# Moving the last batch's third and fourth X and its Fourier products one part later between the first feed-forward products

## The chip, the cores and the metric

The kernel runs on one core of a Trainium2 chip. The metric is the device time of one execution in microseconds (us). TensorE (PE) does the matrix products and the transposes, PEld is its loading of weights, VectorE is DVE, ScalarE is ACT, GpSimd is POOL, and SyncE (SP) issues most of the DMAs.

## The reference

Two blocks follow each other, all in float32 (the two weight matrices arrive as float64 and are converted on the chip). The first is attention whose heads are mixed before and after the softmax; its result is laid out as rows of 768 values. The second adds to each batch the real part of a Fourier transform over the sequence and over the model width, normalises each row, and applies a feed-forward block.

```
scores = einsum('bhij,hg->bgij', scale * q @ k.T, w_pre)      # batch 8, heads 12, seq 448, dim 64
attn   = softmax(scores)
attn   = einsum('bhij,hg->bgij', attn, w_post)
x      = (attn @ v) as rows (8, 448, 768)
u      = x + real(fft(fft(x, axis=1), axis=2))
un     = (u - mean) / sqrt(var + 1e-6)
out    = u + relu(un @ w_ch1) @ w_ch2                         # 768 -> 3072 -> 768
```

## The kernel before, in words

The kernel has two phases, `mix_phase` and `ffn_phase`.

**The mixing loop.** A batch is cut into 23 steps (GS = 23), so eight batches make TOT = 184 steps; the last batch begins at step f = 161. In a step PE mixes the heads before the softmax (`mx`, L704), VectorE takes the maximum, ScalarE the exponential, POOL scales by the sum, PE mixes again (`po`, L738), VectorE transposes. Work that is not bound to one step lies in lists with due step numbers (`due`, `take`): among them the products with v (`emit_av`, L769), which ScalarE copies into the tile `XT`.

**X, the folds, the Fourier products.** For each batch there are four groups of rows. `emit_x` (L813) transposes a group's `XT` into the tile X by six PE transposes and two ScalarE copies (L516). The groups come in the order of the table AT_X, whose entries are a step and a group number: 0, 1, 3, 2; they are called the first to the fourth X here. Since the Fourier matrices are symmetric, rows and columns are first added to and subtracted from their mirror images on POOL: `fold` puts eight small calls per pair of groups on a list (L834, L839, L848, L849), and after the second pair four more that join the two pairs into `xf` (L855). In the loop the folds are taken a few at a time. A Fourier product over the sequence (`emit_z`, four per batch, L878) needs all of `xf`: whatever folds are still on the list are issued in front of it, and PE then waits for POOL. ScalarE copies its result to `z`. A second product over the width (`emit_s2`, four per batch, L894) follows, whose result VectorE adds to X in four additions (L905, L907), and when both halves are there the rows of `u` are stored in DRAM: by SP (L926), by POOL with an indirect DMA (L917) and one last row by POOL (L923).

**What does not fit into the loop.** For the last batch the late items cannot be hidden under a following batch. `mix_phase` returns them as a list of parts, in the order of their due steps, each with a call that issues it, and a call `fold_rest(n)` that issues the next n folds. A part whose due step is from TOT + 10 = 194 on also first issues the stores that are pending (the list `later`).

**The feed-forward phase** works on seven tiles of 512 rows and six parts of the weights. Each tile has a first and a second half, each of seven products (a product scheme with seven instead of eight, in the order 0, 4, 5, 1, 6, 2, 3). In `first`, each product is six matmuls (L1264) of a `ub` tile (the transposed, normalised rows and their sums; the buffers are named qs, ks or ub) with a weight tile `w1t`, into the PSUM banks psP, psQ or psR; VectorE and ScalarE combine the results to `h` (L1274 to L1293), and VectorE makes sums of `h` (L1310, L1311, L1314, L1325) at the end. In `second`, each product is four matmuls (L1341) of `h` with `w2t`, which VectorE adds to the rows (`ur`, `u`, L1346). While tile t runs, tile t + 1 is prepared: VectorE takes statistics (L1182), POOL turns them into scale and bias in four steps (`power`, L440 to L443, tile `mv`), ScalarE normalises (L1193), PE transposes (L1202), ScalarE copies (L1204) into the next `ub` tiles. SP loads `u` (L1161), `w1t` (L1165) and `w2t` (L1169) and stores the `ub` tiles of tile 0 (L1498).

**The parts in between.** The function `next_part` takes one part from the list. It is called in tile 0 behind the first and second product of `first`, then behind the fourth to seventh product of `second`, and in tile 1 behind the first, fourth, fifth, sixth and seventh product of `first`: eleven times. Behind the second product of tile 0 six folds are issued with `fold_rest(6)`, behind its sixth product all others. The order on PE, DVE, POOL and SP is the order of the code here (`manual_schedule`), and that on ScalarE is a scheduler's; each engine carries out its instructions in its order.

The lines that set which items are left for the parts are the due step of an X of the last batch, and the end of the loop:

```
            at, gi = AT_X[n]
            if b == B - 1 and n > 1:
                at += 2
            due("full", f + at, lambda g=groups[b * NG + gi]: emit_x(g))
...
        while s <= TOT - GS + AT_X[-1][0]:
```

With AT_X = ((17, 0), (23, 1), (28, 3), (31, 2)) the last batch's third X is due at 161 + 30 = 191 and its fourth at 194. The loop runs to 161 + 31 = 192. So the third X is in the loop and the fourth is the first of ten parts.

Of the kernel before, what the change touches and what calls it, by code (L numbers as in the profile page):

```python
# [45 lines left out]
GS = BLOCK_AT[-1]  # L46
# [14 lines left out]
TOT = B * GS  # L61
# [36 lines left out]
         (11, 11, 12), (12, 15, 14))  # L98
AT_AV = ((6, 9, 10), (13, 13, 14), (19, 19, 22), (24, 26, 27))
AT_X = ((17, 0), (23, 1), (28, 3), (31, 2))  # L100
AT_Z = (38, 38, 40, 40)
AT_S = ((41, 44), (47, 48))

# [374 lines left out]
def mix_phase(ctx, tc, rest, ident, q, k, v, w_pre, w_post, u_scr, u_rev, wts, lead):  # L478
# [39 lines left out]
    def flush():  # L518
        while pend:
            pend.pop(0)[1]()  # L520
# [63 lines left out]
    def emit_load_qk(b, xx, nm, y):  # L584

        src = q if nm == "q" else k
        if y == 0 and b == 0 and xx == START[-1]:

            if "raw" not in first:
                first["raw"] = ppv.tile([P, GT, 2 * S], F32, name="Pv", tag="Pv")  # L590
            batches[b]["raw" + nm, xx] = first["raw"][:, nm == "q"].rearrange(
                "p (c x d) -> p c x d", c=C7, x=2)
        elif y == 0:
            batches[b]["raw" + nm, xx] = praw.tile([P, C7, 2, D], F32, name="raw" + nm,
                                                   tag="raw")
        t = batches[b]["raw" + nm, xx]
        for x in range(2):
            eng = nc.gpsimd if b else (nc.sync, nc.scalar if xx == START[0] else nc.gpsimd)[x]
            eng.dma_start(
                out=t[64 * y:64 * y + 64, :, x, :],  # L600
                in_=src[b, 4 * xx + 2 * x + y].rearrange("(p c) d -> p c d", c=C7))
        return True
# [35 lines left out]
    def emit_xpose(b, xx, nm):  # L638
        st = batches[b]
        raw = st.pop(("raw" + nm, xx))  # L640
        w = WQ if nm == "q" else S
        t = pqt.tile([P, 2, w], F32, name=nm + "T", tag=nm + "T")
        st[nm + "T", xx] = t
        rt = _row(t)
        if nm == "q":
            eng = nc.gpsimd if b else nc.vector
            eng.memset(t[:, :, 0:MG], 0.0)
            eng.memset(t[:, :, MG + S:WQ], 0.0)
        evs = []
        for c0, n in ((0, 4), (4, 3)):  # L650
            ps = ms_tile()
            for c in range(n):
                nc.tensor.transpose(
                    ps[:, c * P:(c + 1) * P],
                    raw[:, c0 + c].rearrange("p x d -> p (x d)"), ident[:, :])
            dst = _ap(t, (w - S) // 2 + c0, [[rt, P], [1, n], [w, 2], [C7, 64]])
            src = ps[:, :n * P].rearrange("p (c y t) -> p c y t", c=n, y=2)
            evs.append(lambda dst=dst, src=src, n=n: copy(ENG["tr", nm, n], dst, src))
        return evs

    def emit_qk(n, xx):

        bk = blocks[n]
        st = batches[bk["b"]]
        engs = ENG["QK"] if n > 1 else "ad"
        if "Sb" not in bk:
            bk["Sb"] = psb.tile([P, 6, S], F32, name="Sb", tag="Sb")
        c0, w = bk["r0"] + MG, R * bk["rs"]
        n = 64 + w
        pss = [ms_tile() for _ in range(2)]  # L670
        for y in range(2):
            for o in (64 * y, 64 * y + 32):
                lo = c0 + o - 64 + (0 if y else w)
                hi = min(lo + 32, c0 + w)
                for x in range(2):
                    nc.tensor.matmul(  # L676
                        pss[x][o:o + hi - lo, :S],
                        st["qT", xx][64 * x:64 * x + 64, y, lo:hi],
                        st["kT", xx][64 * x:64 * x + 64, y, :],
                        start=True, stop=True)  # L680
        return [lambda x=x: copy(engs[x], bk["Sb"][:n, 2 * xx + x, :],
                                 pss[x][:n, :S]) for x in range(2)]
# [251 lines left out]
    def due(kind, at, fn):  # L934
        fill[kind].append((at, len(fill[kind]), fn))
# [4 lines left out]
    for b in range(B):  # L940
        f = b * GS
        at_t = [(a, nm, xx) for xx, at in enumerate(AT_T) for nm, a in zip("qk", at)]
        if b == 0:

            for i, xx in enumerate(START):
                for j, nm in enumerate("kq"):
                    for y in range(2):
                        due("none", -40, lambda xx=xx, nm=nm, y=y: emit_load_qk(0, xx, nm, y))
                    due("full", 2 * i + j - 20, lambda xx=xx, nm=nm: emit_xpose(0, xx, nm))
                for n, at in enumerate((2 * i - 18, i - 13)):  # L950
                    due("QK", at, lambda n=n, xx=xx: (emit_qk(n, xx), n))
            for pr in range(3):
                for y in range(2):
                    due("none", -40, lambda pr=pr, y=y: emit_load_v(0, pr, y))
        else:
            f0 = f - GS
            for n, (a, nm, xx) in enumerate(sorted(at_t, key=lambda e: e[0])):
                at, a = (AT_L[n], a) if b > 1 else (AT_L1[n], AT_T1[n])
                for y in range(2):
                    due("none", f0 + at[y],  # L960
                        lambda b=b, xx=xx, nm=nm, y=y: emit_load_rows(b, xx, nm, y))
                due("flip", f0 + a, lambda b=b, xx=xx, nm=nm: emit_flip(b, xx, nm))
        for pr in range(3 if b else 0):
            for y in range(2):
                due("none", f + AT_V[pr][y], lambda b=b, pr=pr, y=y: emit_load_v(b, pr, y))
        for n in range(0 if b else 2, NBL):
            for xx in range(3):
                due("QK", AT_QK0[n][xx] if b == 0 and n in AT_QK0 else
                    f + AT_QK[n][xx] - (GS if n < 3 else 0),
                    lambda n=NBL * b + n, xx=xx: (emit_qk(n, xx), n))  # L970
        for n in range(NG):
            for pr in range(3):
                due("AV", f + AT_AV[n][pr],
                    lambda a=b * NG + n, pr=pr: (emit_av(a, pr), None))
            at, gi = AT_X[n]
            if b == B - 1 and n > 1:
                at += 2
            due("full", f + at, lambda g=groups[b * NG + gi]: emit_x(g))
        for n, at in enumerate(AT_Z):
            due("full", f + at, lambda b=b, n=n: emit_z(b, n // 2, n % 2))  # L980
        for pair in range(2):
            for par in range(2):
                due("full", f + AT_S[pair][par],
                    lambda b=b, pair=pair, par=par: emit_s2(b, pair, par))
    f = (B - 1) * GS
# [35 lines left out]
    s = int(min(v_[0][0] for v_ in fill.values()))  # L1021
    ET = mybir.EngineType
    with tc.manual_schedule(engines={ET.PE, ET.DVE, ET.Activation, ET.Pool}):
        while s <= TOT - GS + AT_X[-1][0]:
            old = len(later)
            n = take("none", s)
            ahead, now = 0 <= s + LM < TOT, 0 <= s < TOT
            for op in ORDERS[ORD[s % GS]]:
                if op == "flush":
                    flush()  # L1030
                elif op in fill:
                    take(op, s)
                elif op == "conv":
                    if s >= 4:
                        wts.deal(1)
                elif op == "gather":
                    if 0 <= s + LG < TOT:
                        if any(e[2] is not None and e[2] <= at_step[s + LG][0] for e in pend):
                            flush()
                        emit_gather(s + LG)  # L1040
                elif op == "scale":
                    if ahead:
                        emit_scale(s + LM)
                    for _ in range(old if s < TOT + 5 else 0):
                        later.pop(0)()

                    if s < TOT - 3:
                        for _ in range(min(len(folds), 1 if n and s > 3 else 2)):
                            folds.pop(0)()
                elif op in ("post", "turn"):  # L1050
                    if now:
                        (emit_postmix if op == "post" else emit_turn)(s)
                elif ahead:
                    (emit_premix if op == "pre" else emit_max if op[0] == "m"
                     else emit_exp)(s + LM, *map(int, op[3:]))
            s += 1
        flush()
        assert not wts.ops
        wts.deal(0)
# [545 lines left out]
```

## Time and profile before

| | us |
|---|---|
| median of 3 runs | 2301.52 |
| lowest and highest of them | 2299.84, 2303.2 |
| the profiled execution's own time | 2302.76 |
| its span, first to last instruction | 2301.0 |
| mean granted TensorE clock | 0.991 |

The profile is of one execution. Times in it are counted from the span's start, so about 1.8 us of the execution's time lie around the span. A row of a time line has the start, the length, the engine, the line, the operation, what it writes and reads, how many instructions it stands for, and in brackets the idle time of the engine ahead of it with what ended it. Matmuls overlap a little, so a row's length is about 0.16 us more than the distance to the start of the next. A line such as L1264 is a line of the kernel before; behind line 100 the changed kernel's lines have numbers one higher.

### The profile page before, as it was taken

Reading aid. Unit: us, or ns where it says so; the run is one execution under the profiler, and the core shown is the slowest. Engines: PE = TensorE matmul, PEld = TensorE weight load, DVE = VectorE, ACT = ScalarE, POOL = GpSimd, SP = SyncE. Lnnn points to the kernel's source line nnn. Section 1 sums busy time; section 2 is a strip of 40 time slices with the busy share of each in tenths; the row PEclk is TensorE's granted clock in tenths of the full one; section 3 lists DMA queues with packets and bytes.
Section 4 is the critical chain, followed back from the end, with each engine's and each line's share of the span. In section 5 each row is a group of like instructions: output and inputs, shape, how many; then the busy total and the mean of one; then the engine's idle time right before and its main releaser. Section 6 shows DMA issues by size and latency. Waiting matters only on the chain. (4 is left out here: it accounts for less than half of the span.)

```text
span 2301.0 us, 60190 instructions
## 1 busy us (share of the span) xinstructions
PE 2235.0 (97%) x22600; PEld 1745.0 (76%) x22600; DVE 1723.4 (75%) x3640; ACT 1141.1 (50%) x3288; POOL 1310.4 (57%) x1805
## 2 busy tenths in 40 slices
PE   6999999999999799999999999999999999999998
PEld 3445555555555567676899999999999999999998
DVE  5778888898888547777777787878778877765545
ACT  4666666667666423231445445444444445434434
POOL 6688888989869522211555455546545645454334
PEclk8999999999999999999999999999999999999999
DMA  7576676666746555658777887878777987795664
GB/s 167 169 186 181 177 198 171 196 182 189 195 152 184 189 181 178 225 186 305 207 178 187 240 220 188 218 185 246 208 187 187 284 184 175 192 255 121 144 147 76
DMA packets 228828, 439.41 MB, mean 191 GB/s; under 512 B 35964, under 2 KB 149558, under 8 KB 228540
## 3 DMA queue, kind: packets, MB, share of 16 engines
q1 hardware_dynamic: 156620, 301.52, 38.5%
q0 software_dynamic: 69632, 133.00, 30.9%
q8 instruction: 181, 2.97, 0.6%
q10 hardware_dynamic: 2288, 1.05, 0.2%
q14 instruction: 107, 0.88, 0.1%
HBM read 213.16 MB, written 143.16 MB: 155 GB/s over the span
## 5 line engine op out<-in xcount | busy, mean ns | idle before, releaser
L1420 POOL DMA_DIRECT2D out_dram<-od x172 | 209.0, 1274 | 260.8 <-DVE od L1408 177.4
L718 ACT ACTIVATE PP<-mx,nmx 128x448 f32<-128x448 f32 x368 | 231.1, 634 | 171.5 <-DVE nmx L711 161.2
L728 POOL TENSOR_SCALAR PP<-PP,rcp 128x448 f32<-128x448 f32 x368 | 234.6, 648 | 138.7 <-DVE rcp L726 105.3
L711 DVE TENSOR_REDUCE nmx<-mx 128x1 f32<-128x448 f32 x368 | 212.6, 615 | 92.1 <-PE mx L704 90.3
L1227 POOL TENSOR_TENSOR hq<-h 128x128 f32<-128x128 f32 (+1 forms) x210 | 130.1, 619 | 255.4 <-ACT h L1286 123.0
L704 PE MATMUL mx<-Kr,kw 60*32 60x448 f32 x2944 | 226.6, 553 | 16.8 <-DMA Kr<-Sb 12.6
L1414 ACT COPY od<-psP 128x192 f32<-128x192 f32 x488 | 156.3, 320 | 171.7 <-PE psP L1386 170.6
L1417 DVE TENSOR_TENSOR od<-od 128x768 f32<-128x768 f32 x210 | 200.5, 968 | 52.5 <-ACT od L1414 52.3
L738 PE MATMUL po<-PP,kw 60*32 60x448 f32 x2944 | 208.4, 541 | 3.1 <-POOL PP L728 2.1
L752 DVE STREAM_TRANSPOSE Pv<-po 128x896 f32<-128x896 f32 x184 | 203.6, 1106 | 8.5 <-PE po L738 5.8
L676 PE MATMUL ms<-kT,qT 64*32 64x448 f32 (+1 forms) x3072 | 196.6, 543 | 3.2 <-ACT qT L516 1.9
L516 ACT COPY Sb<-ms 124x448 f32<-124x448 f32 (+1 forms) x378 | 178.7, 546 | 40.9 <-PE ms L676 28.0
L769 PEld LDWEIGHTS ms<-Pv,vv 64*64 64x64 f32 x5376 | 139.9, 133 | 63.4 <-issue 34.6
L1264 PE MATMUL psP<-ks,w1t 128*128 128x256 f32 x744 | 179.9, 380 | 0.1
L1264 PE MATMUL psP<-qs,w1t 128*128 128x256 f32 x744 | 179.0, 379 | 0.7 <-DVE h L1285 0.7
L769 PE MATMUL ms<-Pv,vv 64*64 64x120 f32 (+1 forms) x5376 | 160.9, 264 | 4.9 <-issue 2.7
L281 POOL TENSOR_SCALAR wst<-wst 128x256 f32<-128x256 f32 (+1 forms) x76 | 118.5, 1567 | 68.5 <-ACT wst L292 67.2
L1264 PEld LDWEIGHTS psP<-ks,w1t 128*128 128x128 f32 x744 | 140.1, 191 | 16.9 <-DVE u L1346 0.7
L1264 PEld LDWEIGHTS psP<-qs,w1t 128*128 128x128 f32 x744 | 139.5, 190 | 17.4 <-DVE h L1285 1.1
L676 PEld LDWEIGHTS ms<-kT,qT 64*32 64x32 f32 (+1 forms) x3072 | 74.1, 106 | 80.6 <-issue 51.4
L1264 PE MATMUL psP<-ub,w1t 128*128 128x256 f32 x528 | 127.1, 379 | 0.6 <-DVE h L1285 0.6
L738 PEld LDWEIGHTS po<-PP,kw 60*32 60x32 f32 x2944 | 71.1, 107 | 72.2 <-issue 54.2
(203 smaller groups left out, 5271.2 us busy)
## 6 DMA issues: line engine op xcount, KB each, us to landing
Kr<-Sb SPq DMA_DIRECT2D x730, 105.0 KB
out_dram<-od POOLq DMA_DIRECT2D x172, 384.0 KB, 7.0
qs<-ub SPq DMA_DIRECT2D x89, 384.0 KB
ks<-ub SPq DMA_DIRECT2D x88, 384.0 KB
ub<-ub SPq DMA_DIRECT2D x79, 384.0 KB
w1t<-w SPq DMA_DIRECT2D x42, 384.0 KB
w2t<-w SPq DMA_DIRECT2D x42, 384.0 KB
raw<-in_moe_w_ch_dram SPq DMA_DIRECT2D x32, 384.0 KB
```

Of the source, the lines that this page charges most:

```text
L516: (nc.scalar.copy if eng == "a" else nc.vector.tensor_copy)(out=out, in_=in_)
L676: nc.tensor.matmul(pss[x][o:o + hi - lo, :S], st["qT", xx][64 * x:64 * x + 64, y, lo:hi], st["kT", xx][64 * x:64 * x + 64, y, :], start=Tr ...
L704: nc.tensor.matmul(mx[x][64 * z + o:64 * z + o + 32, :S], kw1[64 * x:64 * x + KR, o:o + 32], Kr[64 * x:64 * x + KR, z, :], start=True, sto ...
L711: nc.vector.tensor_reduce(nmx[:, :], steps[T]["mx"][x][:, :S], axis=AX.X, op=ALU.max, negate=True)
L718: nc.scalar.activation(steps[T]["PP"][:, x, :], steps[T]["mx"][x][:, :S], ACTF.Exp, bias=steps[T]["nmx", x][:, :], accum_out=steps[T]["den ...
L728: nc.gpsimd.tensor_scalar(PP[:, x, :], PP[:, x, :], rcp[:, x:x + 1], 1.0, op0=ALU.mult, op1=ALU.mult)
L738: nc.tensor.matmul(po[o:o + 32, z, :S], kw2[64 * z:64 * z + KR, y, :], _ap(PP, 64 * z * _row(PP) + 32 * c, [[_row(PP), KR], [S, 2], [64, C ...
L752: nc.vector.transpose(turned[a]["Pv"][:, j, :].rearrange("p (z s) -> p z s", z=2), steps[T]["po"][:, :, :S])
L769: nc.tensor.matmul(pss[y][64 * x:64 * x + 64, :nu * R], st["v", pr][64 * y:64 * y + 64, x, jb * D:(jb + 1) * D], _ap(Pv, 64 * y * rp + 32 ...
L1264: mm = nc.tensor.matmul(p[:, m, :], w1[i][:, kc, m * P:(m + 1) * P], ub[:, kc, :], start=i in (0, 4, 1)[:3 - seed] and m == kc == 0, stop= ...
L1417: eng.tensor_tensor(D[j][:, :, :], D[j][:, :, :], D[k][:, :, :], op=ALU.add)
L1420: nc.gpsimd.dma_start(out=acc[t, r, d], in_=D[j][:, :, :], accum_op=ALU.add)
```

## The change

The last batch's third and fourth X are now due at TOT + AT_END and the step after (191 and 192), with AT_END = 7, and the loop ends ahead of step TOT + AT_END. Its last step is 190, so both are parts, and there are eleven. Since both have due steps below TOT + 10, neither issues pending stores first.

```
+AT_END = 7
...
             at, gi = AT_X[n]
             if b == B - 1 and n > 1:
-                at += 2
+                at = TOT - f + AT_END + n - 2
             due("full", f + at, lambda g=groups[b * NG + gi]: emit_x(g))
...
-        while s <= TOT - GS + AT_X[-1][0]:
+        while s < TOT + AT_END:
```

What this moves is seen in the order of the instructions. First PE, from the end of the mixing loop on, before (L769 is the last product with v, L813 an X, L1264 feed-forward products of tile 0, L878 a Fourier product):

```order
L769 MATMUL ms<-Pv,vv 64x120 x56
L813 MATMUL ms<-ident,XT 113x128 x6
L1264 MATMUL psP<-qs,w1t 128x256 x6
L813 MATMUL ms<-ident,XT 113x128 x6
L1264 MATMUL psR<-qs,w1t 128x256 x6
L878 MATMUL ms<-ts,xf 97x113
L878 MATMUL ms<-ts,xf 97x112
L878 MATMUL ms<-ts,xf 97x113
L878 MATMUL ms<-ts,xf 97x112
L1264 MATMUL psP<-ks,w1t 128x256 x6
L1264 MATMUL psQ<-qs,w1t 128x256 x6
```

And the same place of the changed kernel (its line numbers are one higher):

```order
L770 MATMUL ms<-Pv,vv 64x120 x56
L1265 MATMUL psP<-qs,w1t 128x256 x6
L814 MATMUL ms<-ident,XT 113x128 x6
L1265 MATMUL psR<-qs,w1t 128x256 x6
L814 MATMUL ms<-ident,XT 113x128 x6
L1265 MATMUL psP<-ks,w1t 128x256 x6
L1265 MATMUL psQ<-qs,w1t 128x256 x6
```

Each X stands behind one more product, and the first Fourier product has left this place; it now stands behind the last transposes (L1203) of the second half of tile 0, where the second one stood before. The trace counts each of these float32 matmuls twice.

On POOL, before, from the indirect store of batch 6 to the weight loads (v is `u`'s store in DRAM, the folds are L834 to L855, mv is the scale and bias of tile 1's rows):

```order
L917 DMA v_79<-X,rows 449x768
L923 DMA v_79<-X 16x1x48
L834 TENSOR_TENSOR xs<-X 113x384 x2
L839 TENSOR_TENSOR xs<-xs 113x383
L848 TENSOR_TENSOR xq<-xs 113x192 x2
L849 COPY xq<-xs 113x1
L834 TENSOR_TENSOR xs<-X 113x384 x2
L839 TENSOR_TENSOR xs<-xs 113x383
L848 TENSOR_TENSOR xq<-xs 113x191 x2
L849 COPY xq<-xs 113x1
L855 TENSOR_TENSOR xf<-xq 113x385 x2
L855 TENSOR_TENSOR xf<-xq 113x383 x2
```

And in the changed kernel:

```order
L918 DMA v_79<-X,rows 449x768
L835 TENSOR_TENSOR xs<-X 113x384 x2
L840 TENSOR_TENSOR xs<-xs 113x383
L849 TENSOR_TENSOR xq<-xs 113x192 x2
L850 COPY xq<-xs 113x1
L835 TENSOR_TENSOR xs<-X 113x384 x2
L441 TENSOR_SCALAR mv<-mv 128x4
L442 TENSOR_TENSOR mv<-mv,mhalf 128x4
L443 TENSOR_TENSOR mv<-mv 128x4
L444 TENSOR_SCALAR mv<-mv 128x4
L840 TENSOR_TENSOR xs<-xs 113x383
L849 TENSOR_TENSOR xq<-xs 113x191 x2
```

The store of batch 6's last row (L923) has gone from ahead of the folds to behind them and behind three of the weight loads (L261) that follow. The four mv steps, which stood behind all twelve folds, stand behind the first six.

On ScalarE, before, around the relus of tile 0's `h` (L1283 to L1293) and the first normalisations (L1193):

```order
L516 COPY z_14923<-ms 97x450
L1278 COPY h<-psP 128x512
L1283 ACTIVATE h<-h 128x512
L1286 ACTIVATE h<-h 128x512
L1193 ACTIVATE un<-u,mv 128x768
L1291 ACTIVATE h<-h 128x512
L1293 ACTIVATE h<-psP 128x512
L1193 ACTIVATE un<-u,mv 128x768
```

And in the changed kernel:

```order
L517 COPY X<-ms 113x384 x2
L1279 COPY h<-psP 128x512
L1284 ACTIVATE h<-h 128x512
L1287 ACTIVATE h<-h 128x512
L1294 ACTIVATE h<-psP 128x512
L1194 ACTIVATE un<-u,mv 128x768
L1292 ACTIVATE h<-h 128x512
L1194 ACTIVATE un<-u,mv 128x768
```

The relu of the seventh product (L1293, one higher now) has moved ahead of the first normalisation. In tile 1 the four groups of VectorE additions (L905, L907) stand one product later each, so that the last group stands behind the sixth product and ahead of the sums of `h` (L1310, L1311). The order on SP is the same in both.

## The prediction

> **What bounds the kernel now.** The page comes first: its head gives the span and how much of it TensorE works.
>
> ```profile
> span 2301.0 us, 60190 instructions
> ...
> PE 2235.0 (97%) x22600; PEld 1745.0 (76%) x22600; DVE 1723.4 (75%) x3640; ACT 1141.1 (50%) x3288; POOL 1310.4 (57%) x1805
> ```
>
> TensorE (PE) is busy for 2235.0 of 2301.0 us, so 66 us at most can be had from its waits. Next is the list of whom PE waits for: total, times, longest.
>
> ```profile
> PE mx L704 <- DMA Kr<-Sb: 12.6, 11, 3.9
> PE ms L878 <- POOL xf L855: 12.6, 2, 12.3
> ```
>
> The first is spread over eleven steps of the mixing loop. The second is almost one wait: 12.3 us for the folded rows `xf` of GpSimd (POOL), before a Fourier product (L878). That line is one that the change moves. The busy time by stretches shows that the place is alone (columns: length, then PE, PEld, DVE, ACT, POOL busy, granted clock, DMA share, GB/s):
>
> ```profile
> 800.00:808.00 8.00, 0.00 (x0) 0.00 (x0) 0.00 (x0) 0.00 (x0) 7.61 (x12) 0.50 0.91 299
> 808.00:812.00 4.00, 3.33 (x12) 2.77 (x13) 0.00 (x0) 0.54 (x1) 3.21 (x4) 0.50 0.75 187
> ...
> 872.00:1572.00 700.00, 695.81 (x3430) 602.53 (x3429) 539.90 (x1172) 282.10 (x723) 297.34 (x377) 1.00 0.75 214
> 1572.00:2290.00 718.00, 717.20 (x3812) 666.91 (x3811) 501.69 (x1064) 327.31 (x912) 353.49 (x428) 1.00 0.74 181
> ```
>
> From 800 to 808 us POOL works alone. When PE resumes, its granted clock is 0.50. From 872 us to nearly the end PE is idle 4.2 + 0.8 = 5.0 us in 1418: what is saved ahead of it is passed on to the end. PE's own time line there:
>
> ```profile
> 789.36 0.91 PE L813 MATMUL ms<-ident,XT 128*113 128x128 f32 x6 [0.80 <-ACT XT L795]
> 790.11 2.76 PE L1264 MATMUL psP<-qs,w1t 128*128 128x256 f32 x12
> 792.70 0.82 PE L813 MATMUL ms<-ident,XT 128*113 128x128 f32 x6
> 793.36 2.76 PE L1264 MATMUL psR<-qs,w1t 128*128 128x256 f32 x12
> 808.41 0.69 PE L878 MATMUL ms<-ts,xf 113*97 113x113 f32 x2 [12.29 <-POOL xf L855]
> 809.36 1.44 PE L878 MATMUL ms<-ts,xf 112*97 112x112 f32 x6 [0.26 <-POOL xf L855]
> 810.60 3.57 PE L1264 MATMUL psP<-ks,w1t 128*128 128x256 f32 x12
> 814.00 2.75 PE L1264 MATMUL psQ<-qs,w1t 128*128 128x256 f32 x12
> ...
> 824.36 1.45 PE L1341 MATMUL psP<-w2t,h 128*128 128x384 f32 x4
> 826.72 1.56 PE L1341 MATMUL psP<-w2t,h 128*128 128x384 f32 x4 [0.91 <-ACT h L1293]
> ...
> 832.86 2.75 PE L1341 MATMUL psP<-w2t,h 128*128 128x384 f32 x8
> ...
> 840.38 0.94 PE L878 MATMUL ms<-ts,xf 113*96 113x113 f32 x8
> 841.16 2.76 PE L1341 MATMUL psP<-w2t,h 128*128 128x384 f32 x8
> ```
>
> The third X (transposes at 789.36), the fourth (792.70) and the first Fourier product (808.41) each stand one feed-forward product apart. Between the fourth X and the Fourier product that needs its folds there is a single product of 2.59 us (790.11 to 792.70 is the pace of one). What POOL has to do in that time:
>
> ```profile
> 787.03 1.60 POOL L839 TENSOR_TENSOR xs<-xs 113x383 f32<-113x383 f32 x1
> 788.71 2.45 POOL L848 TENSOR_TENSOR xq<-xs 113x191 f32<-113x191 f32 x2
> ...
> 798.01 0.56 POOL L923 DMA_DIRECT2D v<-X  x1 [4.83 <-DMA v<-X,rows]
> 798.60 1.94 POOL L834 TENSOR_TENSOR xs<-X 113x384 f32<-113x384 f32 x2
> 800.62 1.00 POOL L839 TENSOR_TENSOR xs<-xs 113x383 f32<-113x383 f32 x1
> 801.69 1.15 POOL L848 TENSOR_TENSOR xq<-xs 113x192 f32<-113x192 f32 x2
> ...
> 807.36 3.85 POOL L855 TENSOR_TENSOR xf<-xq 113x385 f32<-113x385 f32 x4
> ...
> 824.37 0.24 POOL L443 TENSOR_SCALAR mv<-mv 128x4 f32<-128x4 f32 x1
> ```
>
> POOL first waits 4.83 us to store a last row (L923, batch 6), then folds from 798.60 to 811.21: 12.6 us.
>
> **The change, part by part.** The step numbers give TOT = 184. The loop, which ran to step 192, ends with 190; the third X, due at 191, leaves it and becomes the first part between the products, and every later part moves back by one place: the fourth X from behind the first product to behind the second, the four Fourier products from (second product; fourth, fifth, sixth of L1341) to the fourth to seventh of L1341, the four L894 steps one place on. Nothing is added or removed: the same matmuls, copies, folds and DMAs.
>
> *The waits.* Counted in the old time line, PE gains: the 0.80 us wait for XT, since a product that waits for nothing late takes that place; 12.29 + 0.26 us for the folds; and the half clock behind them. Under it the first Fourier product took 810.60 − 808.41 − 0.26 = 1.93 us, against 841.16 − 840.38 = 0.78 for its like at full clock, 1.15 saved; and the product at 810.60 took 3.40 to the next start against 2.59, 0.81 saved. Without a long idle time I take the clock as 1.00 throughout.
>
> *ScalarE's order.* The relu of the seventh product (L1293) now stands ahead of the first normalisation (L1193) and not behind it and another relu. The rows of before:
>
> ```profile
> 793.39 0.87 ACT L516 COPY X<-ms 113x384 f32<-113x384 f32 x2
> ...
> 824.64 1.03 ACT L1193 ACTIVATE un<-u,mv 128x768 f32<-128x768 f32 x1 [3.84 <-POOL mv L443]
> ...
> 826.10 0.57 ACT L1293 ACTIVATE h<-psP 128x512 f32<-128x512 f32 x1
> ```
>
> It ended at 826.67, and PE waited 0.91 us for it. Call T the end of the seventh product (824.36 of before). The relu can now be done by T + 0.8, and PE needs its bank at T + 1.3: 0.91 saved. Sum: 0.80 + 12.55 + 1.15 + 0.81 + 0.91 = 16.22 us.
>
> *What is late next.* In the new order T is 788.56 + 7 × 2.59 + 2 × 0.66 = 808.0. The fourth X's transposes end at 795.1, ScalarE's copies (0.87) at about 796.1; L923, which POOL waited with, has gone behind the folds and three weight loads. POOL then does six of twelve folds, the four `mv` steps (L440 to L443), and the other six. The last six are an L839, an L848 and the L855 rows, 1.00 + 1.15 + 3.85 = 6.0 us; of the 8.76 us ahead of L855 two rows each of 1.94, 1.00 and 1.15 leave 0.6 for small copies and gaps, half of it theirs: 6.3, and as much for the first six. These are done by 802.4. In before `mv` ended at 824.61 = T + 0.25; its chain from the fifth product over VectorE is unchanged, so 808.3, and the first folds do not hold it. The normalisation that follows the relu ends at T + 1.9, ahead of the transposes at T + 2.6. The other folds are done at 814.6. The first Fourier product comes at T + 16.0 − 0.9, about 823.1, so cover is 8.5 us.
>
> *VectorE beside POOL* is the unknown cost. In before VectorE is idle while the last folds run. Now they run beside the sums of `h` (L1310 to L1325) that PE's second to sixth products of L1341 read. What such company costs, beside a lone example of the same size (851.17):
>
> ```profile
> 787.81 1.64 DVE L473 TENSOR_TENSOR ks<-ks,qs 128x768 f32<-128x768 f32 x1
> ...
> 826.22 0.69 DVE L1310 TENSOR_TENSOR h<-h 128x512 f32<-128x512 f32 x1 [3.22 <-ACT h L1291]
> ...
> 830.26 0.56 DVE L1346 TENSOR_TENSOR ur<-ur,psR 128x384 f32<-128x384 f32 x1 [0.49 <-PE psR L1341]
> ...
> 851.17 0.95 DVE L1209 TENSOR_TENSOR qs<-qs,ks 128x768 f32<-128x768 f32 x1
> ```
>
> An addition went from 0.95 to 1.64 us, and POOL's L839 and L848 from 1.00 and 1.15 to 1.60 and 2.45 us. From below, 0: the first sum waits for the second relu (as long as L1293's 0.57, so T + 2.4), ends at T + 3.1, and PE asks for it at T + 2.59 + 0.66 = T + 3.3. From above, each of the four sums is longer by the worst row's 0.69 us: the first ends at T + 3.8, PE stands 0.5; the accumulator read behind the fourth (0.56, L1346), which frees a bank for PE's third product (832.86, that is T + 7.6 without the 0.91), ends at T + 2.4 + 4 × 1.38 + 0.56 = T + 8.5, and PE stands 0.4 more: 0.9. I take 0.3, since the first sum has 0.2 us of room and the others over 1.
>
> The Trainium skill ("SBUF — State Buffer", section "Who interferes with whom") says that VectorE instructions with two SBUF inputs and GpSimd ones that read SBUF share a port that is locked, so that the later one stands fully blocked rather than being slowed. Rows agree as far as the fold at 788.71 grew by more than an addition's whole lone time. By that rule each sum could wait for a whole POOL instruction; its price, worked out from rows, is the first rival.
>
> *DMA.* SyncE's order is unchanged, and its transfers do not move with PE:
>
> ```profile
> SPq L1161 <- DMA w2t<-w: 5.9, 6, 1.6
> ...
> 806.54 1.45 SPq L1161 DMA_DIRECT2D u<-v  x2
> ...
> 809.76 0.90 SPq L1498 DMA_DIRECT2D ub<-qs  x2
> ...
> 833.99 0.97 ACT L1204 COPY qs<-psQ 128x384 f32<-128x384 f32 x2
> ```
>
> SyncE's loads of `u` waited six times for a `w2t` to land; the last such pause ends at 806.54, so all of `w2t` has landed before T = 808.0: no wait. The stores of the old `ub` tiles (L1498) are issued from 809.76 on, as now. The first ScalarE copy into a slot that such a store reads is that at 833.99 = T + 9.6; it comes at 808.0 + 9.6 − 0.9 = 816.7, still 7 us behind that store's issue. I take 0.
>
> *Second tile.* One group of four VectorE additions (L905, L907) now stands ahead of its `h` sums. Each has half the columns of the 0.95 us addition, some 1.9 us for all by that; PE needs the first sum only after its seventh product, one of L1341 and transposes, 2.59 + 2.59 + 0.66 = 5.8 us. Nothing is lost.
>
> So 16.2 − 0.3 = 15.9 us is saved. The profiled execution took 2302.76 us and would take 2286.9; the median of the runs shown, 2301.52, lies 1.24 below it, so 2285.6 is forecast.
>
> **Rivals.**
>
> *The lock.* Each of the four sums waits for one of POOL's 0.96 us instructions (3.85 / 4) and then takes 0.69: the first ends at T + 4.1, PE stands 0.8 us; the accumulator read ends at T + 9.6 against 7.6 + 0.8, 1.2 more: 2.0 us, and 0.1 for what follows. For: the grown rows. Against: they grew less than that on the mean. Gain 16.2 − 2.1 = 14.1: 2287.4. Chance 0.14.
>
> *The stores collide.* POOL's weight loads now fall into the time of the `ub` stores. The seven tiles (128 × 3 × 256 floats, 393 KB) are 2.75 MB, 9.2 us at the 299 GB/s of the first stretch above. If the first store counts as landed only when all have (819.0), ScalarE and then PE stand 2.3 us: gain 16.2 − 0.3 − 2.3 = 13.6, 2287.9. For: a DMA share of 0.75 to 0.91 there. Against: they leave in the order in which they are needed. Chance 0.08.
>
> *Slower: the wait comes back, longer.* PE takes its work in order; at the first Fourier product, now at 823.1, it stands until POOL has done the second six folds, which begin only behind `mv` at 808.3. They have 14.8 us for 6.3 of lone work: up to a growth by 2.3 nothing is lost (the worst pair of rows, 2.45 to 1.15, is 2.1). At 2.6 the wait is 1.6 us; at 5.0 it is 16.7, the whole gain, and the change does nothing; at 6.0 PE stands 23.0 us and comes back at half clock (1.15 + 0.81 more): 25.0 − 16.2 = 8.8 us slower, 2310.3. VectorE would have to hold POOL almost without a pause, for which no row speaks. Chance 0.03, and 0.02 for a growth about 5, where the change does not do what it says.
>
> **How the numbers follow.** The forecast keeps 0.73. The range holds it with both bounds and the two faster rivals: its lower end, 2283.0, is the shown runs' lowest, 2299.84, less the full 16.2 and a little; its upper end, 2290.0, is the highest, 2303.2, less the 13.6 us of the store rival, rounded up. Runs of this kernel lie within 3.4 us, 0.15%, so 0.2% (4.6 us) is about what can be told from no change. Faster by more: 0.73 + 0.14 + 0.08 = 0.95; within 0.02; slower 0.03.
>
> **What would show it.** In the new profile: no PE wait for `xf` over 1 us and the clock at 1.00 from 780 to 860; PE's first L1264 product at about 788.6 and first L1341 product at 808; POOL's folds starting at 796 with `mv` among them; PE's wait for L1293 gone. A PE wait on VectorE's `h` sums or accumulators of 1 us or more shows the lock; ScalarE waiting for a `ub` store shows the collision. I am wrong if PE's idle time between 786 and 872 has fallen by less than 11 us, or if the time after 872 has grown.

## The result, and the profile after

The changed kernel took 2289.83 us (median of 5 runs, 2286.9 to 2293.59), the kernel before beside it 2301.52 us (2299.84 to 2305.26). The ratio is 0.9946 with a 95% interval of 0.9931 to 0.9961: faster by 9 to 16 us. The profiled execution took 2286.9 us, 15.86 less than that of before; its page begins so:

```profile
span 2285.1 us, 60189 instructions
...
PE 2229.7 (98%) x22600; PEld 1743.3 (76%) x22600; DVE 1724.5 (75%) x3640; ACT 1140.7 (50%) x3288; POOL 1309.0 (57%) x1805
```

PE's busy time fell by 5.3 us, though it carries out as much: 2.1 us of it in the stretch below, where the half clock is gone, and 3.1 us in the first 786 us, in which executions differ. First the stretch with the moved parts, by busy time. Before:

```profile
786.00:872.00 86.00, 70.22 (x388) 56.00 (x379) 42.87 (x85) 21.39 (x43) 28.97 (x39) 0.92 0.61 204
```

And after, 16 us shorter, with the stretch behind it:

```profile
786.00:856.00 70.00, 68.10 (x377) 54.86 (x372) 43.93 (x82) 21.87 (x44) 29.58 (x38) 1.00 0.77 249
856.00:1556.00 700.00, 695.74 (x3429) 602.47 (x3428) 540.48 (x1175) 281.22 (x722) 298.08 (x378) 1.00 0.75 215
```

PE's idle time there went from 15.8 to 1.9 us and the granted clock from 0.92 to 1.00. The 700 us behind it have 4.3 us of idle time against 4.2. PE's time line shows what became of each wait:

```profile
788.21 2.86 PE L1265 MATMUL psP<-qs,w1t 128*128 128x256 f32 x12
790.90 0.82 PE L814 MATMUL ms<-ident,XT 128*113 128x128 f32 x6
791.55 2.76 PE L1265 MATMUL psR<-qs,w1t 128*128 128x256 f32 x12
794.15 0.82 PE L814 MATMUL ms<-ident,XT 128*113 128x128 f32 x6
794.80 2.75 PE L1265 MATMUL psP<-ks,w1t 128*128 128x256 f32 x12
...
807.75 2.74 PE L1342 MATMUL psP<-w2t,h 128*128 128x384 f32 x8
...
815.61 2.85 PE L1342 MATMUL psP<-w2t,h 128*128 128x384 f32 x8 [0.37 <-DVE ur L1347]
...
823.23 0.94 PE L879 MATMUL ms<-ts,xf 113*97 113x113 f32 x8
824.01 2.76 PE L1342 MATMUL psP<-w2t,h 128*128 128x384 f32 x8
...
857.53 2.74 PE L1342 MATMUL psP<-w2t,h 128*128 128x384 f32 x8
```

The first product starts without a wait, the first L1342 product at 807.75 is one piece of eight matmuls (no wait for the relu inside it), and the first Fourier product at 823.23 waits for nothing. One wait is new: 0.37 us for VectorE's accumulator read. POOL, ScalarE and VectorE in the same place, in this order:

```profile
795.46 1.95 POOL L835 TENSOR_TENSOR xs<-X 113x384 f32<-113x384 f32 x2 [2.62 <-ACT X L517]
...
806.00 0.25 POOL L441 TENSOR_SCALAR mv<-mv 128x4 f32<-128x4 f32 x1 [4.12 <-PE psR L1265]
...
810.12 0.65 POOL L850 COPY xq<-xs 113x1 f32<-113x1 f32 x1
810.73 5.22 POOL L856 TENSOR_TENSOR xf<-xq 113x385 f32<-113x385 f32 x4
```

```profile
807.96 0.60 ACT L1294 ACTIVATE h<-psP 128x512 f32<-128x512 f32 x1 [3.76 <-PE psP L1265]
808.45 1.02 ACT L1194 ACTIVATE un<-u,mv 128x768 f32<-128x768 f32 x1
```

```profile
810.02 0.71 DVE L1311 TENSOR_TENSOR h<-h 128x512 f32<-128x512 f32 x1 [3.63 <-ACT h L1292]
810.76 1.52 DVE L1312 TENSOR_TENSOR h<-h 128x512 f32<-128x512 f32 x1
...
813.61 1.48 DVE L1326 TENSOR_TENSOR h<-h 128x512 f32<-128x512 f32 x1
```

The folds start at 795.46 and end at 815.95, 7.3 us ahead of the Fourier product. Three of the four sums of `h` take 1.5 us beside them, where before one took 0.69, and POOL's L856 rows 5.22 us where before they took 3.85. The first sum stood beside a small copy of the folds (L850): the sum took 0.71 us, and the copy 0.65 where before it took 0.19.

### The profile page after: what moved, and what is told of

It reads as the page before. It is cut to its first block, busy times and chain, and to the rows that moved or that the text cites. A ratio compares the mean times of both kernels' runs of the same rounds, so it can differ in the third digit from the quotient of the medians.

```text
span 2285.1 us, 60189 instructions
## 1 busy us (share of the span) xinstructions
PE 2229.7 (98%) x22600; PEld 1743.3 (76%) x22600; DVE 1724.5 (75%) x3640; ACT 1140.7 (50%) x3288; POOL 1309.0 (57%) x1805
## 3 DMA queue, kind: packets, MB, share of 16 engines
q10 hardware_dynamic: 2288, 1.05, 0.2%
```

## The experiments

The question was whether the 15.9 us of the profile or the 11.7 us of the medians is what the change does, and which of its parts does it. Each run is read by three lengths of its profile, since executions of one kernel differ by some us in the mixing loop: the head, up to the end of the last product with v (L769; 788.57 before); N, from there to the first L1341 product of tile 1 (873.88 − 788.57 = 85.31 before, 857.53 − 788.27 = 69.26 after), at which PE is done with all moved parts in each kernel; and the tail behind. M of the expectations is N and the tail together. Each row is one profiled execution, so N of before rests on a single profile; store_ahead, fold_5_more, fold_12_more, warm_30 and folds_ahead were executed once and are read by their profiles alone.

| kernel | head | N | tail |
|---|---|---|---|
| before | 788.57 | 85.31 | 1427.12 |
| changed, first | 788.27 | 69.26 | 1427.57 |
| after_again | 793.46 | 69.25 | 1427.79 |
| after_third | 787.39 | 69.23 | 1428.68 |
| z_later_only | 794.10 | 70.09 | 1427.51 |
| z_later_again | 789.29 | 70.11 | 1429.10 |
| x_later_only | 792.30 | 86.99 | 1427.31 |
| warm_clock | 787.14 | 87.31 | 1426.65 |
| warm_30 | 790.36 | 85.13 | 1427.71 |
| store_ahead | 782.86 | 69.24 | 1427.50 |
| fold_5_more | 784.44 | 68.61 | 1428.15 |
| fold_12_more | 785.09 | 72.99 | 1428.82 |
| folds_ahead | 786.05 | 70.31 | 1428.64 |

**after_again.** The changed kernel without an edit. Expected:

> The changed kernel as it is, timed and profiled again. Theory A (the gain lies wholly between 786 and 856 us of the span and is the same in every execution, about 15.9 us; the first comparison's 11.7 us is less because executions differ by some us in the mixing loop ahead of it): PE idle about 2 us between 786 and 856 again; the stretch behind it as long as before's to 0.5 us; what differs from the first profile lies ahead of 786; the ratio's interval takes in 0.9931. Theory B (the new order costs about 4 us in most executions that the first profile happened not to show): 4 us more idle time behind 786, ratio about 0.995.

Median 2290.7 us (8 runs, 2283.22 to 2298.82), before 2302.33 (25 runs, 2291.44 to 2316.01), ratio 0.9938 (0.9910 to 0.9966). N is 69.25, the same to 0.01 us; the head is 5.2 us longer. In the first 780 us, PE's waits for the gathered rows of the mixing loop were, in the first profile:

```profile
PE mx L705 <- DMA Kr<-Sb: 9.7, 9, 3.9
```

and in this one:

```profile
PE mx L705 <- DMA Kr<-Sb: 13.7, 13, 4.5
```

This wait alone is 4.0 us longer; others of the loop differ by up to about 3 us, both ways. Theory A holds: N and, to 0.2 us, the tail are as in the first profile.

**z_later_only.** Before, with an empty part:

```diff
+    parts_out.insert(1, lambda t: None)
```

> Before, with an empty part behind the fourth X, so that the Fourier products move one part later while both X, the loop's end and the row store ahead of the folds stay. Theory A (the wait for the folds in front of the first Fourier product is what was paid): the 0.80 us wait for XT stays, the folds start at about 798.5 and are done by 816, before 823; no wait for xf; gain 15.0 us, about 2286.5. Rival (the earlier end of the loop, with both X behind products, is what pays): little gain, under 4 us.

PE waits for XT as before, and no longer for `xf`:

```profile
794.90 0.91 PE L813 MATMUL ms<-ident,XT 128*113 128x128 f32 x6 [0.80 <-ACT XT L795]
...
829.89 0.94 PE L878 MATMUL ms<-ts,xf 113*97 113x113 f32 x8
```

N is 70.09, a gain of 15.2 us, 0.85 less than the changed kernel's: the XT wait. The Fourier products' place alone is worth nearly everything. The timed median was 2282.89 (6 runs, 2277.62 to 2293.45), ratio 0.9899 (0.9871 to 0.9928), lower than N lets expect, which led to a repeat below.

**x_later_only.** The changed kernel with the first Fourier product in the fourth X's part:

```diff
+    x4, z1 = parts_out[1:3]
+    parts_out[1:3] = [lambda t: (x4(t), z1(t))]
```

> The changed kernel with the first Fourier product joined to the fourth X's part, so that both X and the loop's end move but the first Fourier product stands where it stood, behind the second feed-forward product (the row store then is issued ahead of the folds again). Theory A: PE waits for xf some 12 to 13 us at about 795 to 808, at half clock behind; gain 0 to 1 us, about 2301. Rival (the loop's end pays): most of the gain stays, under 2292.

```profile
812.34 0.69 PE L879 MATMUL ms<-ts,xf 113*97 113x113 f32 x2 [13.36 <-POOL xf L856]
...
814.53 4.14 PE L1268 MATMUL psP<-ks,w1t 128*128 128x256 f32 x12
...
832.14 1.56 PE L1345 MATMUL psP<-w2t,h 128*128 128x384 f32 x4 [1.82 <-ACT h L1297]
...
834.19 2.75 PE L1345 MATMUL psR<-w2t,h 128*128 128x384 f32 x8
```

Ratio 0.9998 (0.9977 to 1.0018): no gain. N is 1.7 us longer than before, where 0 to 1 less was expected. The XT wait is gone, but POOL sets the end of the wait, 0.2 us later; the product behind it starts 3.98 us ahead of the next (3.40 before) at half clock; and ScalarE's scheduler put two normalisations ahead of the relu, a wait of 1.82 for 0.91. The rival, that the loop's earlier end pays, falls. The 1.82 us wait left the clock alone: the whole product behind it (834.19) takes 2.75, as at full clock.

**warm_clock and warm_30.** Before, with 26 and then 30 matmuls ahead of the first Fourier product, whose result nobody reads:

```diff
+WARM = 26
...
+                if n == 0 and k == 1:
+                    idle = ppx.tile([P, 512], F32, name="ms", tag="ms")
+                    for _ in range(WARM):
+                        nc.tensor.matmul(idle[:, :HT], w1[i][:, 0, :P], ub[:, 0, :],
+                                         start=True, stop=True)
                 next_part()
```

> Before, with 26 matmuls of 128x256 (11.2 us) whose result nobody reads put on PE ahead of the first Fourier product, in the time in which it waits for the folds. Theory A (of the 16.2 us, 1.96 are the half clock after the wait): the wait is filled, the clock stays at 1.00, the first Fourier product takes 0.78 and the product behind it 2.59; gain 2.0 us, about 2299.5, folds done at 811 as before. Rival (the clock does not fall because PE is idle, or costs nothing): gain 0.

```profile
807.77 0.43 PE L878 MATMUL ms<-ts,xf 113*97 113x113 f32 x2 [1.85 <-POOL xf L855]
808.72 0.82 PE L878 MATMUL ms<-ts,xf 112*97 112x112 f32 x6 [0.52 <-POOL xf L855]
809.38 4.45 PE L1265 MATMUL psP<-ks,w1t 128*128 128x256 f32 x12
```

Ratio 0.9997 (0.9978 to 1.0015), and N 2.0 us longer, where theory A had 2.0 less. The 26 matmuls ended early, and 1.85 + 0.52 us of waiting sufficed for the clock to fall: the product takes 4.29 us to the next start. The two normalisations ahead of the relu cost 0.9 us here too, and the folds began 0.8 us later behind the last product with v than in before. So the run did not do what it was for, and 30 matmuls followed.

> As warm_clock, with 30 matmuls (13.0 us) and not 26, which left PE idle for 1.85 and 0.5 us and saw the clock fall to 0.5 at 809.4 all the same. Theory A: the wait is filled, the clock stays at 1.00, the first Fourier product takes 0.78 and the product behind it 2.59 us; against that ScalarE's order has two normalisations ahead of the seventh product's relu here, 0.9 us more wait than in before: M = 1512.4 - 1.96 + 0.9 = 1511.3, to within 0.5. Rival (the clock falls for another cause than PE's idle time): product at 3.4 us or more, M = 1513.

```profile
811.44 0.82 PE L878 MATMUL ms<-ts,xf 112*97 112x112 f32 x6 [0.38 <-POOL xf L855]
812.10 2.77 PE L1265 MATMUL psP<-ks,w1t 128*128 128x256 f32 x12
```

Now the product takes 2.60 us (812.10 to the next at 814.70) and the Fourier product 1.40 with its wait against 2.19: 0.80 + 0.79 = 1.59 us are the clock's in this place. The expected 1.96 set the Fourier product against a like that runs unbroken in 0.78 us. Here it is broken by a wait for the next `xf` row: this wait is 0.38 us where it was 0.26, and beside it the product takes 1.02 us, 0.24 more than unbroken. N fell by 0.18 only, since 0.9 went to the relu, and the folds were 0.3 and the matmuls' end another 0.2 us later; M, 1512.84, is 1.5 above the expectation, of which 0.6 is the tail, which differs by as much between other executions. With PE kept at work the granted clock stays at 1.00 from 797 to 815, so in this place it is PE's idle time that lowers it.

**store_ahead.** The changed kernel with the row store ahead of the folds:

```diff
-    return fold_rest, [lambda t, fn=fn, at=at: part(fn, t, at < TOT + 10)
+    return fold_rest, [lambda t, fn=fn, at=at: part(fn, t, at < TOT + 8)
```

> The changed kernel with the store of batch 6's last row ahead of the folds again. Measured by the time from the end of the last product with v to the end of the span, M (before 1512.4 us, changed 1496.8), since what lies ahead of it differs by some us from execution to execution. Theory A (from the folds' end at 816.0 to the first Fourier product at 823.2 there are 7 us of cover in the changed kernel): the first six folds start about 3 us later, end ahead of the mv steps still, M = 1496.8 to within 0.5. Rival (each us of POOL ahead of the Fourier product costs one, so that half of the gain came from the store's move): M = 1500 or more.

```profile
792.92 0.57 POOL L924 DMA_DIRECT2D v<-X  x1 [5.15 <-ACT h L1279]
793.51 1.95 POOL L835 TENSOR_TENSOR xs<-X 113x384 f32<-113x384 f32 x2
...
800.59 0.25 POOL L441 TENSOR_SCALAR mv<-mv 128x4 f32<-128x4 f32 x1 [0.66 <-PE psR L1265]
```

POOL's idle time ahead of `mv` shrinks from 4.12 to 0.66 us and takes the delay up whole. N is 69.24 and M 1496.74, as theory A had it: the store's move is worth nothing as long as the Fourier products stand late.

**fold_5_more and fold_12_more.** The changed kernel with 5 and 12 more POOL instructions behind the eighth call of the folds and ahead of `xf`:

```diff
+DOSE = 5
...
+        def more():
+            xs = box[-1]
+            for _ in range(DOSE):
+                pl.tensor_tensor(xs[:, :DH - 1], xs[:, :DH - 1], xs[:, :DH - 1],
+                                 op=ALU.subtract)
+
+        if pair and g["b"] == B - 1:
+            folds.append(more)
```

> The changed kernel with five more POOL subtractions of 113x383 (1.0 us each alone) behind the eleventh small call of the folds and ahead of xf; they work on a tile whose content is no longer needed. Theory A (7 us of cover): xf later by 5 to 6.5 us, no PE wait for it, M = 1496.8 to within 0.5. Rival (no cover: the wait begins at once): M up by 5.

```profile
812.52 3.88 POOL L857 TENSOR_TENSOR xf<-xq 113x385 f32<-113x385 f32 x4
```

```profile
818.75 0.94 PE L888 MATMUL ms<-ts,xf 113*97 113x113 f32 x8
```

`xf` ends at 816.40, 2.35 us ahead of its reader: no wait, M 1496.76. N is 0.65 us shorter still, since the extra instructions change which of POOL's instructions meet VectorE's sums, two of which now take 0.7 us, and the 0.37 us wait is gone.

> The same with twelve of them. Theory A: xf is later by 12 to 13.5 us, that is 5 to 6.5 us behind the cover's end; PE waits that long in front of the first Fourier product and loses 1 to 2 us more to the half clock behind it: M = 1503 to 1505. Rival (the folds' cover is longer than the profile shows, or PE finds other work): M under 1500.

```profile
821.25 0.44 PE L888 MATMUL ms<-ts,xf 113*97 113x113 f32 x2 [1.69 <-POOL xf L857]
822.21 0.82 PE L888 MATMUL ms<-ts,xf 112*97 112x112 f32 x6 [0.52 <-POOL xf L857]
822.87 4.45 PE L1351 MATMUL psP<-w2t,h 128*128 128x384 f32 x8
```

The wait comes back, 2.21 us, and the product behind it takes 4.28 us to the next start (827.15) against 2.59: N is 3.7 us above the changed kernel's. M is 1501.8, below the expected 1503 to 1505. The twelve instructions took 0.99 us each, and the expectation counted up to the last `xf` row, while PE starts with the first: it started at 821.25, 2.8 us ahead of the end of the last (824.06). So the wait was 2.2 and not 5 us. Between 5 and 12 lies the edge, as theory A had it.

**folds_ahead.** All twelve folds ahead of `mv`:

```diff
-                    fold_rest(6)
+                    fold_rest()
```

> The changed kernel with all twelve folds ahead of the mv steps and not six. Theory A (mv is what the normalisation waits for, and VectorE's sums are slowed by the folds beside them): mv ends about 1.5 us later (809.5 on the changed profile's clock), the sums of h take 0.6 us each again and the 0.37 us wait for the accumulator read goes, while PE waits about 1 us for the normalised rows: M = 1497.3, to within 0.6. Rival (neither matters): M = 1496.5 or less with the 0.37 us gone.

```profile
809.11 0.88 PE L1203 MATMUL psQ<-ident,un 128*128 128x128 f32 x6 [0.83 <-ACT un L1194]
810.35 2.85 PE L1342 MATMUL psR<-w2t,h 128*128 128x384 f32 x8 [0.37 <-DVE h L1311]
```

VectorE's sums, alone now, take the time of before:

```profile
809.60 0.69 DVE L1311 TENSOR_TENSOR h<-h 128x512 f32<-128x512 f32 x1 [5.44 <-ACT h L1292]
...
811.54 0.69 DVE L1326 TENSOR_TENSOR h<-h 128x512 f32<-128x512 f32 x1
```

PE waits 0.83 us for the normalised rows and 0.37 for the first sum; the wait for the accumulator read is gone. N is 70.31, 1.05 above the changed kernel's (0.4 to 0.5 was expected: the late first sum was left out). M is 1498.95, outside the expected 1497.3 to within 0.6; the tail is 1.07 of the 2.1 us by which it exceeds the changed kernel's.

**z_later_again and after_third**, on one chip:

> The kernel of z_later_only once more, beside the changed kernel on one chip. Its first timing (ratio 0.990) was below the changed kernel's (0.994), while M, the time from the last product with v to the end of the span, was 0.8 us longer (1497.6 against 1496.8). Theory A (what follows the mixing loop is the same in every execution, and timed medians differ by some us through the loop ahead of it): M = 1497.6 to within 0.5 again, and timed medians within 5 us of the changed kernel's, with either ahead. Rival (this order is truly faster by several us): median lower than the changed kernel's by 5 us or more again.

> The changed kernel a third time, for the comparison with z_later_again. Theory A: M = 1496.8 to within 0.5, ratio to before in 0.991 to 0.996. Rival: M or the ratio differs from the two earlier ones by more.

Medians 2288.85 (6 runs, 2282.25 to 2291.91), ratio 0.9927 (0.9900 to 0.9953), and 2286.6 (6 runs, 2283.21 to 2292.18), ratio 0.9922 (0.9896 to 0.9948); before 2303.07. N is 70.11 and 69.23, as at first. M came out at 1499.2 and 1497.9, off by 1.6 and 1.1, all of it in the tail (1429.10 and 1428.68), so M was too coarse a measure. The order of the two medians has turned round, and their intervals overlap: that z_later_only is truly faster is not borne out. Which part of the executions made its first timing short is not shown, since the only one of those runs with a profile was the slowest (2293.45, head 794.10).

## Why the prediction was right, and where it was not

- **The waits.** Confirmed as worked out: the 0.80 us for XT (z_later_only keeps it and is 0.85 us longer), the 12.55 us for the folds, gone because the Fourier products stand behind four L1341 products (z_later_only alone gains 15.2 us, x_later_only nothing).
- **The half clock.** The changed kernel stays at 1.00. Of the 1.96 us, 1.59 are seen in before's place with PE kept busy. The rest, 0.37, belongs to the break in the first Fourier product (a longer wait for `xf`, 0.12, and a slower run, 0.24), and with the products moved it goes as well. The sum is right, its parts were named wrongly.
- **ScalarE's order.** Confirmed: PE no longer waits for the relu (0.91 us); where the scheduler put two normalisations ahead of it, the wait was 1.82.
- **T, the folds, `mv`.** T was worked out as 808.0 with a head of 788.56 and came at 807.75 with 788.27, the same; the folds' end, as 814.6, came at 815.95, and the cover is 7.3 and not 8.5 us. Both count to the last of the four `xf` rows; PE's first Fourier product waited in before for the first two alone (it started at 808.41 and ran on at 809.36, POOL ended at 811.21), so there is more room than that.
- **VectorE beside POOL.** 0.3 us was taken and 0.37 came, but not where it was put. The first sum, with 0.2 us of room, kept its length, and the fold copy beside it grew instead; the other three grew from 0.69 to 1.5 us, more than the 1.38 of the upper bound, and the accumulator read behind them was late. By the rival of the lock each sum takes 0.96 + 0.69 = 1.65; three of four came near it, so as a mechanism it was the better description. The rival's price of 2.1 us had the first sum late as well; that 0.37 came instead is luck in so far as only a short copy was left beside that sum. In this the trace agrees with what the Trainium skill says in "SBUF — State Buffer", section "Who interferes with whom": of a VectorE instruction with two SBUF inputs and a GpSimd one that reads SBUF, the later is blocked. The copy went from 0.19 to 0.65 us and ended when the sum did; the reads of PSUM (L1347, with one SBUF input) were not longer than before.
- **DMA.** No ScalarE copy waited for a store of `ub`: that rival falls.
- **Second tile.** PE's first L1342 product there (857.53) waits for nothing: the additions ahead of the sums of `h` cost nothing, as taken.
- **The wait that comes back.** fold_12_more shows it as a mechanism: once the cover is used up, PE waits and loses the clock as well. The changed kernel is more than five POOL instructions away from it.
- **The sum.** 15.9 us forecast, 16.05 in N (85.31 to 69.26), three times alike to 0.03 us, and 15.86 between the profiled executions. **What failed** is the step from the profiled execution to the median. It took 2301.52 less 15.9; the measured median is 4.2 us above that. The prediction treated the loop ahead as fixed, and the range of three runs (3.4 us) as the spread. In later comparisons runs of before went from 2291 to 2316 us, and in the profiles the head went from 782.9 to 794.1 and the tail from 1426.7 to 1429.1 us. The three comparisons gave 0.9946, 0.9938 and 0.9922; 16.05 us are 0.9930, within the second and third interval and 0.0001 below the first. That the first five runs were 4 us slower through their heads is likely but not shown, since four of them have no profile. The median stands only 0.17 us inside the range, whose upper end, 2290.0, had been drawn for the rival of the stores; that rival did not come, so that the range held the median is luck.
- **What is passed on to the end.** The prediction took the time behind 872 us as unchanged, and growth there as a sign of being wrong. From N's end on it grew by 0.45 us between the first profiles. Over all profiles the tail is 1426.7 to 1427.7 us (mean 1427.2) in the four with the first Fourier product in its old place and 1427.5 to 1429.1 us (mean 1428.2) in the nine with it moved. Much of the spread is one PE wait some 235 us behind N's end, for VectorE's L1285: 0.71 us in before, 0.82 in the first profile of the changed kernel and 1.93 in z_later_again. Whether the moved order causes it is not shown; if it does, about 1 of the 16.05 us is given back.

No version was found that beats the changed kernel by more than can be timed: fold_5_more's N is 0.65 us shorter, 0.03%, by instructions that compute nothing.

## What to carry to other kernels

Where an engine that works in order waits for a long chain on another engine, look for independent work that the reader can be moved behind: z_later_only moved the readers alone and gained 15.2 of 16.05 us, while x_later_only, which moved both X later and left the reader where it was, gained nothing. Moving the chain earlier was not tried: in before POOL stood 4.83 us for a store ahead of the folds. Set against the cover the chain's time and what it will be slowed by its new neighbours, and look whether what now falls beside it (three sums at 1.5 us) has room. To tell gains of 0.5% where executions differ by as much, compare the length between two fixed instructions in the profiles: N repeated to 0.03 us where medians moved by 4.

## What the runs showed of the hardware

- A short wait can cost PE more than itself. After 1.69 + 0.52 us of waiting in fold_12_more the granted clock fell to 0.50, which added 1.7 us; after 1.85 + 0.52 in warm_clock it added 1.7 too (rows above). The clock in fold_12_more:

```profile
821.00:822.80 1.80, 1.03 (x8) 0.84 (x9) 0.00 (x0) 0.00 (x0) 1.80 (x3) 1.00 0.03 7
822.80:824.00 1.20, 1.20 (x6) 0.80 (x5) 0.00 (x0) 0.53 (x1) 1.20 (x2) 0.76 0.00 0
824.00:826.00 2.00, 2.00 (x4) 1.00 (x3) 0.56 (x1) 0.00 (x0) 1.99 (x5) 0.50 0.24 43
```

  It falls when PE is already at work again, at about 823.4: the penalty belongs to a wait that is over. Not every such wait pays it: behind the single 1.82 us wait in x_later_only the clock stayed at 1.00. Where the limit lies is not shown.
- Additions with two SBUF inputs on VectorE and tensor instructions on POOL hinder each other in both directions: 0.69 to 1.5 us for a sum, 3.85 to 5.22 for four L856. In folds_ahead, without company, both had their old lengths.
